# An attention kernel with a mixture of adapters behind it: one ring of four PSUM banks, casts tied to vector steps that read PSUM, and reordered first loads and mixture slots

## The chip, the cores and the metric

The kernel runs on one core of a Trainium2 chip. The metric is the device time of one execution in microseconds (us). Most executions of one kernel lie within 1 or 2% of each other. A run more than 1.5% above the fastest run of the same kernel is called slow and is left out of ratios. The profiled span is about 1.7 us shorter than the time of the same run, because the span runs from the first to the last instruction only.

Engines in the profile: PE is the matrix engine, PEld its weight load, DVE the vector engine, ACT the scalar engine, POOL the GpSimd engine and SP the engine that issues most transfers. A name with a q behind it (SPq, ACTq) is that engine's instruction stream issuing a transfer. The program keeps PE's results in tiles of PSUM, counted in banks, and its other tiles on the chip in SBUF. A transfer has landed when its semaphore tells that the data is there.

## The reference

The input is q, k and v of shape (8 batches, 8 heads, 576, 64), a table of biases, and the weights of a mixture of eight adapters.

```python
scores = q @ k.T / sqrt(64) + bias_table[bucket(|i - j|)]      # per batch and head
attn   = softmax(scores)
x      = (attn @ v), heads side by side                        # (4608, 512)
logits = x @ w_gate                                            # (4608, 8)
topk   = the two largest logits; w = softmax of these two
out    = x + sum over the two of  w_e * (x @ A[e]) @ B[e]      # rank 16
```

## The kernel before

The work is cut into 32 pairs (8 batches, four pairs of heads each) of five score groups. The bias is applied after the exponential, as a multiplication of a band of the probabilities ("band"). The 64 rows that 576 leaves over 512 are handled as "tails". Per pair: casts of k and q to bf16 on Pool, transposes on PE, scores on PE, exponentials on ACT, bands on DVE, values ("pv") on PE, and normalization into x on DVE. When the four pairs of a batch are done, the batch goes through the mixture while the next batch's attention runs: x is transposed by a DMA transfer (x to xT), then PE computes the logits (lp), the gate follows, and PE computes z and the output.

The parts that matter here, with cuts marked:

```python
scp = tile_pool("sc_ps",  bufs=2, space=PSUM)   # scores, two banks each
pvp = tile_pool("pv_ps",  bufs=1, space=PSUM)   # values: ONE buffer of two banks
acp = tile_pool("acc_ps", bufs=2, space=PSUM)   # transposes, mixture
...
def cast_kq(i, w, eng=None):                    # free-running on Pool
    ...
    nc.gpsimd.tensor_copy(o, s)
...
def norm(i, between):                           # frees the pv buffer at its end
    nc.vector.reciprocal(rc, at(acc, D, (SLOT, 5), (D1, 2)))
    between()                                   # a band
    nc.vector.tensor_tensor(rm, rc, mask, op=ALU.mult)
    nc.vector.tensor_tensor(xs[b][:, :, 2*hp:2*hp+2, :], <acc>, <rm>, op=ALU.mult)
...
def m_xdma(b):                                  # 512 KB, issued by SP in its order
    nc.sync.dma_start_transpose(out=xT, in_=xs[b][:, 0:4]...)
...
def mixture(b):
    i0 = HP * (b + 1) + 1                       # HP = 4 pairs per batch
    at_slot(0, 0, lambda: m_xdma(b))            # second pair of the next batch, group 0
    at_slot(1, 1, lambda: m_logits(...))        # six groups later
    ...
for i in range(NPAIR + 1):
    b, hp = divmod(i, HP)
    if hp == 0 and b + 1 < B:
        load_kq(b + 1, 0, H)                    # SP: k and q of the next batch, 1 MB each
        load_tails(b + 1)
    if b + 1 < B:
        load_v(b + 1, (hp,))                    # SP: four 64 KB transfers per pair
    ...
```

The softmax here doesn't subtract the row's maximum and nothing guards it: scores larger than these inputs give would overflow.

## Time and profile before

The median of the time before was 255.85 us over three runs. The page of the profile gives busy times per engine; the share is of the span. No engine is full, so the time is made of waits in turn.

The head of the page of the kernel before:

```profile
span 254.5 us, 6519 instructions
## 1 busy us (share of the span) xinstructions
PE 187.8 (74%) x2496; PEld 123.7 (49%) x2496; DVE 195.0 (77%) x483; ACT 162.7 (64%) x184; POOL 117.3 (46%) x229
```

What matters, read from the start of each pair's first exponential in the timeline:

| stretch | us |
|---|---|
| first exponential | 12.0 |
| start of pair 4 | 47.4 |
| pairs 4 to 30, each | 6.67 |
| from the start of pair 31 to the end | 26.9 |

The waits view lists who stood, for whom, in all, how often, and the longest. These are lines of the kernel before; PE waits for DVE to free the value buffer, for xT to land, and once for a long time for the first casts:

```profile
engine line waited for: us in total, times, longest us
...
PE pv L366 <- DVE x L392: 12.5, 13, 1.9
PE lp L438 <- DMA xT<-x: 11.9, 6, 3.1
...
PE kqps L287 <- POOL kqn L132: 10.0, 2, 7.3
```

The groups view by form gives busy time and mean of one instruction. On DVE, the three band sizes and the small multiplication rm:

```profile
L350 DVE TENSOR_TENSOR p<-p,M 128x768 bf16<-128x768 bf16 x64 | 38.4, 609 | 0.6 <-ACT p L335 0.5
L350 DVE TENSOR_TENSOR p<-p,M 128x512 bf16<-128x512 bf16 x64 | 29.3, 458 | 2.7 <-POOL M L223 2.7
...
L342 DVE TENSOR_TENSOR p<-p,M 128x256 bf16<-128x256 bf16 x32 | 18.5, 579 | 0.1
L391 DVE TENSOR_TENSOR rm<-rc,mask 128x10 f32<-128x10 f32 x32 | 10.2, 319 | 0.0
```

A band of 128x256 takes 579 ns on average, more than one of twice the size (458). The median of that form is 283 ns, so a few are very long. The timeline shows one; columns are start, duration, engine, line and operation. This is the one on DVE:

```profile
107.83 2.20 DVE L342 TENSOR_TENSOR p<-p,M 128x256 bf16<-128x256 bf16 x1
```
And this is the timeline of Pool over the same time, in the same columns:

```profile
107.58 0.64 POOL L132 CAST kqn<-kf 128x512 bf16<-128x512 f32 x1
108.14 0.63 POOL L132 CAST kqn<-qf 128x512 bf16<-128x512 f32 x1
108.69 0.63 POOL L137 CAST vn<-vf 128x512 bf16<-128x512 f32 x1
109.26 0.62 POOL L132 CAST kqn<-kf 128x512 bf16<-128x512 f32 x1
```

The band of 2.20 us lies over Pool's casts, which read SBUF. It ends at 110.03 us, while Pool's next cast (109.81 to 110.49 us) still runs. Take for each form of DVE instruction (with at least four of a form) the time above the form's 10th percentile: 27.4 us in all. The 62 instructions with two inputs in SBUF that overlap a Pool cast hold 23.7 us of it, the 45 with an input in PSUM that overlap one hold 0.05 us. This is what the change means to remove.

### The profile page before, as it was taken

How to read it: one execution, taken by the hardware profiler on the slowest of the kernel's cores; microseconds unless marked ns; L12 is line 12 of the kernel's file. 1: busy time of each engine (PE TensorE's matmuls, PEld its weight loads, DVE VectorE, ACT ScalarE, POOL GpSimd, SP SyncE). 2: the span in 40 equal slices, each digit the busy share in tenths (PEclk: the TensorE clock that was granted, in tenths of full speed). 3: DMA queues.
4: the chain of work that ended last, by engine and by line, in shares of the span. 5: the costliest groups of instructions: out<-in, count | busy, mean ns of one | idle time of the engine just before them, and what ended most of it. 6: DMA issues, size and time to landing. Idle time of an engine off the chain costs nothing.

```text
span 254.5 us, 6519 instructions
## 1 busy us (share of the span) xinstructions
PE 187.8 (74%) x2496; PEld 123.7 (49%) x2496; DVE 195.0 (77%) x483; ACT 162.7 (64%) x184; POOL 117.3 (46%) x229
## 2 busy tenths in 40 slices
PE   1324965888987596869879898879784997897650
PEld 1102543655754473546646574547353675556510
DVE  5215673899999579897997698988998599798771
ACT  3251874689987485777876586769676487895000
POOL 8599928671835254334743282714452282020100
PEclk9999998899999889899997797999889599999965
DMA  7999996997988697596987693886967301910616
GB/s 163 148 128 271 273 97 146 308 150 153 322 108 199 135 292 113 128 186 157 324 155 166 166 304 38 183 175 198 244 152 162 74 0 38 213 45 3 165 36 170
DMA packets 91830, 41.28 MB, mean 162 GB/s; under 512 B 69648, under 2 KB 87064, under 8 KB 91800
## 3 DMA queue, kind: packets, MB, share of 16 engines
q1 hardware_dynamic: 74392, 38.77, 61.5%
q0 software_dynamic: 17408, 2.10, 14.8%
q8 instruction: 19, 0.31, 0.5%
q14 instruction: 11, 0.09, 0.1%
HBM read 29.84 MB, written 9.45 MB: 154 GB/s over the span
## 4 chain that ended last, share of the span: by engine, by line
PE 43%; DVE 32%; DMA 13%; POOL 7%; issue 2%; ACT 1%; DVEq 0%; POOLq 0%; ACTq 0%
PE pv L366 17%; DMA xT<-x 11%; PE sc L323 9%; DVE p L350 6%; DVE x L392 6%; DVE o L517 5%; PE zp L487 3%; DVE p L342 3%; DMA tl<-in_q_dram 3%; DVE rm L391 3%; PE dl L513 3%; PE kqps L287 3%; DVE kqT L289 2%; POOL vn L152 2%; DVE tlT L298 2%
## 5 line engine op out<-in xcount | busy, mean ns | idle before, releaser
L335 ACT ACTIVATE p<-sc 128x1024 bf16<-128x1024 f32 x160 | 155.8, 1024 | 65.7 <-PE sc L323 36.1
L366 PE MATMUL pv<-vn,p 128*128 128x65 bf16 (+1 forms) x1152 | 68.2, 206 | 12.6 <-DVE x L392 12.5
L366 PEld LDWEIGHTS <-p 128*128 128x128 bf16 x1280 | 59.0, 104 | 37.4 <-issue 18.9
L350 DVE TENSOR_TENSOR p<-p,M 128x512 bf16<-128x512 bf16 (+1 forms) x128 | 66.2, 533 | 3.3 <-POOL M L223 2.7
L323 PE MATMUL sc<-kqT 64*128 64x512 bf16 x256 | 54.0, 419 | 2.8 <-ACT p L335 2.8
L287 PE MATMUL kqps<-ident,kqn 128*128 128x128 bf16 x256 | 21.6, 229 | 17.0 <-POOL kqn L132 10.0
L366 PE MATMUL pv<-vt,p 128*128 128x130 bf16 x128 | 29.8, 232 | 2.4 <-DVE p L342 2.4
L453 POOL TENSOR_TENSOR df<-lg,m 128x32 f32<-128x32 f32 (+1 forms) x12 | 3.5, 293 | 60.6 <-DVE lg L443 31.8
L287 PEld LDWEIGHTS <-kqn 128*128 128x128 bf16 x256 | 15.8, 101 | 24.6 <-POOL kqn L132 11.3
L392 DVE TENSOR_TENSOR x<-pv,rm 128x640 bf16<-128x640 f32 x32 | 26.4, 825 | 1.1
L289 DVE COPY kqT<-kqps 128x1024 bf16<-128x1024 bf16 x32 | 21.8, 682 | 7.0 <-PE kqps L287 7.0
L117 POOL DMA_DIRECT2D vt<-in_v_dram x16 | 9.8, 621 | 32.6 <-PE pv L366 32.6
L517 DVE TENSOR_TENSOR o<-dl,x 128x512 f32<-128x512 f32 x32 | 21.7, 687 | 3.7 <-PE dl L513 2.7
L323 PEld LDWEIGHTS <-kqT 64*128 64x128 bf16 x256 | 12.8, 94 | 18.5 <-issue 7.3
L132 POOL CAST kqn<-kf 128x512 bf16<-128x512 f32 x31 | 21.1, 680 | 0.1
L132 POOL CAST kqn<-qf 128x512 bf16<-128x512 f32 x31 | 20.5, 662 | 0.0
L137 POOL CAST vn<-vf 128x512 bf16<-128x512 f32 x28 | 20.5, 733 | 0.0
L342 DVE TENSOR_TENSOR p<-p,M 128x256 bf16<-128x256 bf16 x32 | 18.5, 579 | 0.1
L513 PE MATMUL dl<-Bb,zT 128*128 128x512 bf16 x32 | 14.2, 452 | 4.4 <-DVE kqT L289 2.5
L327 PE MATMUL sc<-kqT,tlT 128*128 128x512 bf16 x32 | 13.7, 427 | 0.0
L331 PE MATMUL sc<-tlT,kqT 128*128 128x128 bf16 x128 | 13.5, 233 | 0.0
L438 PE MATMUL lp<-Wb,xT 128*128 128x8 bf16 x128 | 4.5, 167 | 11.9 <-DMA xT<-x 11.9
(85 smaller groups left out, 209.3 us busy)
## 6 DMA issues: line engine op xcount, KB each, us to landing
out_dram<-o SPq DMA_DIRECT2D x64, 128.0 KB, 2.3
kf<-in_k_dram SPq DMA_DIRECT2D x7, 1024.0 KB, 5.9
qf<-in_q_dram SPq DMA_DIRECT2D x7, 1024.0 KB, 10.2
vf<-in_v_dram SPq DMA_DIRECT2D x112, 64.0 KB, 2.9
kf<-in_k_dram SPq DMA_DIRECT2D x4, 256.0 KB, 4.5
qf<-in_q_dram SPq DMA_DIRECT2D x4, 256.0 KB, 4.4
out_dram<-ot SPq DMA_DIRECT2D x8, 128.0 KB, 2.6
tl<-in_k_dram POOLq DMA_DIRECT2D x16, 32.0 KB, 6.8
```

The lines of the kernel that those rows point to most:

```text
L132: (eng or nc.gpsimd).tensor_copy(o, s)
L137: nc.gpsimd.tensor_copy(vns[b % 2][:, :, h, :D], vfs[b][:, :, h, :])
L287: nc.tensor.transpose(o[:, :, j, :], n[:, w, j], ident)
L289: nc.vector.tensor_copy(t, ps)
L323: nc.tensor.matmul(sc[:, h * 512:(h + 1) * 512], lhsT=t[s, 0, g * 128:(g + 1) * 128], rhs=t[s, 1, :], start=True, stop=True)
L335: nc.scalar.activation(p, sc, ACT.Exp, scale=scale)
L342: nc.vector.tensor_tensor(p[:, 384:640], p[:, 384:640], M4[:, hp, :], op=ALU.mult)
L350: nc.vector.tensor_tensor(o, o, Mh[:, :, x0 * 128:(x0 + b1 - b0) * 128], op=ALU.mult)
L366: nc.tensor.matmul(acc[:, sl * SLOT + o:sl * SLOT + o + n], lhsT=lhsT, rhs=rhs, start=start, stop=stop, skip_group_check=True)
L392: nc.vector.tensor_tensor(xs[b][:, :, 2 * hp:2 * hp + 2, :], at(acc, 0, (SLOT, 5), (D1, 2), (1, D)), rm.unsqueeze(3).to_broadcast((128, 5, ...
L513: nc.tensor.matmul(ps, lhsT=zT[:, t, :], rhs=Bb, start=True, stop=True)
L517: nc.vector.tensor_tensor(o[:, t], ps, xs[b][:, t].rearrange("p h d -> p (h d)"), op=ALU.add)
```

## The change: its intent and the diff

The intent has five parts.

1. Pool's casts of k, q and v are each made to wait for one DVE instruction whose successor reads PSUM, so that a cast does not meet a DVE step with two SBUF inputs.
2. The value buffer of two banks becomes two tiles of one bank each out of a ring of four, which transposes and mixture share. Each of the two is normalized and freed separately.
3. Scores are issued one group ahead of their exponential.
4. First loads: v of batch 0 is loaded by ACT and SP instead of Pool, casts of the first pairs go to DVE, and the exponential of the bias table and its transfer to memory (g_d, from which the bias matrix is read) come before the casts.
5. The mixture's slots move; all of one batch's tiles are handled together. xT is requested at group 4 of the first pair (before: group 0 of the second), the logits come at group 0 of the third pair (before: group 1). The distance stays six groups. The loads of a next batch are spread anew as well: eight of v's transfers instead of four in the first pair, and the tails of q one pair later than those of k (before: both in the first pair).

The core of the diff, with cuts:

```diff
-    pvp = tile_pool("pv_ps", bufs=1, space=PSUM)
-    acp = tile_pool("acc_ps", bufs=2, space=PSUM)
+    acp = tile_pool("acc_ps", bufs=4, space=PSUM)
...
+    def behind_dve(inst):
+        tc.add_manual_dep(inst.ins, dve.last.ins.name, ...,
+            reason="reads SBUF beside an instruction with an input in PSUM")
...
-    load_kq(0, 0, 2)
     nc.sync.dma_start(out=btT, in_=bias_table...)
+    load_kq(0, 0, 2)
+    load_v(0, (0, 1), nc.scalar)            # eight transfers issued by ACT
...
-    nc.sync.dma_start(out=g_d.ap(), in_=ge)
+    nc.scalar.dma_start(out=g_d.ap(), in_=ge)
+    cast_kq(0, 0, dve); cast_kq(0, 1, nc.scalar); cast_kq(1, 0, dve); cast_kq(1, 1, dve)
...
 def pv(i, sl):
-        if sl == 0:
-            pvs[i] = pvp.tile([128, 2 * S4], FP32, name="pv", tag="pv")
+        k = sl % 3
+        if k == 0:
+            pvs[(i, sl // 3)] = acp.tile([128, 3, 2 * D1], FP32, name="pv", tag="acc")
...
 def mixture(b):
-        i0 = HP * (b + 1) + 1
+        i0 = HP * (b + 1)
-            at_slot(0, 0, lambda: m_xdma(b))
-        at_slot(1, 1, lambda: m_logits(...))
+            at_slot(0, 4, m_xdma, b)
+        at_slot(2, 0, m_logits, b)
...
-            if b + 1 < B:
-                load_v(b + 1, (hp,))
+            for j in ((0, 1), (2,), (3,), ())[hp]:     # eight v transfers in the first pair
+                load_v(nb, (j,))
...
-                if g in (1, 2) and i + 2 < NPAIR:
-                    cast_kq(i + 2, g - 1)
+            if 3 <= i + 2 < NPAIR:
+                behind_dve(cast_kq(i + 2, 0))
+        if g == 2 and 3 <= i + 2 < NPAIR:
+            behind_dve(cast_kq(i + 2, 1))
+        if g == 4 and HP <= i + 1 < NPAIR:
+            behind_dve(cast_v(i + 1))
```

## The prediction

> **What bounds it now.** No single engine. The busy table gives DVE 195.0 us (77% of 254.5), PE 187.8, ACT 162.7. The ACT timeline: first exponential at 12.0 us, pair 4 of 32 only at 47.4; then 6.67 us a pair until pair 31 at 227.6; last pair and tail 26.9 us.
>
> Floors of one steady pair, summed from start-to-start times of uncontended instructions in the timeline: ACT five exponentials at about 0.92 = 4.8 us; PE 4.9 us at full clock (5.2 at the mean clock 0.92); DVE 4.9 us. So 6.67 holds about 1.5 us of stalls. From the waits and groups views:
> - PE stands behind the transposed x (about 12 us over 6 batches) and behind `x<-pv` freeing the single pv buffer (12.5 us).
> - DVE is held by Pool casts: the band 128x256 has median 283 ns but mean 579 and longest 2512 ns; 10-element rm has median 164, longest 1953. A 2.2 us band at 107.8 lies over four Pool casts. Summed excess over the 10th percentile of each form: about 26 us. This agrees with the Trainium skill, "SBUF — State Buffer", section "Who interferes with whom": a DVE instruction with two SBUF inputs contends with a GpSimd one that reads SBUF, and the loser blocks.
> - Start: PE waits 7.3 us for the kqn casts of pair 1, behind v loads on Pool.
>
> **What changes.**
> 1. Casts follow a DVE step whose successor reads PSUM (0.60 us kqT copy; 0.47 and 0.34 estimated for the two x halves). Casts of 0.61 fit under the first; the other two overrun by 0.15 and 0.3 us. I expect 26 us of excess to fall to 8 to 14.
> 2. The norm is split: one more reciprocal (0.12), two x instead of one (0.81 against 0.74): DVE +0.19 us per pair, +6 us in all.
> 3. PSUM ring of four: pv becomes two one-bank tiles, freed separately; the 12.5 us wait mostly goes, and DVE's wait for transposes falls.
> 4. Scores one group ahead of the exponential: ACT gaps shrink from 1.4 us a pair to about 0.8.
> 5. xT to logits remains about six groups; at 5.7 us a pair this just covers the 4.4 us transfer, so its wait falls from 2 to below 1 us per batch.
> 6. Start: casts of pairs 0 to 2 move from Pool to DVE (0.43 us each), v is loaded by hardware queues. ACT starts near 9 to 10 us and runs pairs 0 and 1 without stop; the bias matrix still lands near 16 to 17 us, behind 2.5 MB of loads. Pair 4 starts near 34 instead of 47.4: about 13 us.
>
> **Sum.** 34 + 27 x 5.75 = 189 for the start of pair 31, plus 25 for the end: 214 us. DVE sets the pair (5.05 floor, 0.4 contention, 0.3 waits), PE close behind. I estimate about 13 us from the start, 25 from the middle, 2 from the end.
>
> Predicted 214 us; 8 in 10: 204 to 227. Faster by over 2%: 0.96; within 2%: 0.03; slower: 0.01.
>
> **What would show it.** Band 256 mean near 300 ns and none over 1.2 us; DVE busy near 180; no `pv<-x` wait on PE; lp wait under 5 us; kqn releasers gone from the start, pair 4 at 32 to 37 us; ACT spacing median under 1.05 us. Wrong if casts still start late (Pool blocked by its own DMA descriptors), hitting bands; if a cast's late end delays the next transposes; if the granted clock drops as PE gets denser; if the bias matrix lands later than 18 us; or if the four-bank ring makes PE wait for DVE in strict order.

## The result, and the profile after

The changed kernel took 238.01 us (median of four runs, 237.07 to 238.95). The kernel before, on the same chip in the same rounds, took 257.74 us (254.53 to 285.35). The ratio of fast runs is 0.933, with a 95% interval of 0.924 to 0.942. A ratio is the mean time of one kernel's fast runs over that of the other's of the same rounds, so it is not quite the ratio of the medians quoted. The change makes the kernel faster by about 7%. The predicted 214 us was too low by 24 us, and the range (204 to 227) did not hold the result.

The head of the page after:

```profile
span 235.5 us, 6536 instructions
## 1 busy us (share of the span) xinstructions
PE 178.6 (76%) x2485; PEld 120.5 (51%) x2496; DVE 185.3 (79%) x540; ACT 160.7 (68%) x180; POOL 101.2 (43%) x195
```

The same stretches as before, beside the prediction, and beside a better version found later (e12, below). All are in us of the profiled span:

| stretch | before | predicted | after | e12 |
|---|---|---|---|---|
| start of pair 4 | 47.4 | 34 | 42.1 | 40.2 |
| 27 pairs | 180.2 (6.67 each) | 155.2 (5.75) | 166.0 (6.15) | 155.2 (5.75) |
| last pair and end | 26.9 | 25 | 27.3 | 27.7 |
| sum | 254.5 | 214 | 235.5 | 223.2 |

The miss in the span is 8 us at the start, 11 us in the middle and 2 us at the end. First, what went as planned. The groups view after (all DVE instructions carry the line of a helper, so the form tells them apart):

```profile
L82 DVE TENSOR_TENSOR p<-p,M 128x768 bf16<-128x768 bf16 x64 | 35.7, 559 | 0.0
...
L82 DVE TENSOR_TENSOR p<-p,M 128x256 bf16<-128x256 bf16 x32 | 12.4, 387 | 0.0
...
L82 DVE TENSOR_TENSOR rm<-rc,mask 128x4 f32<-128x4 f32 x32 | 5.3, 164 | 1.2
```

The band of 256 fell from 579 to 387 ns and its longest from 2512 to 573 ns; rm fell from 319 to 164 ns (it has 4 elements now instead of 10, but its median was 164 before too). Counted as above, the time over each form's 10th percentile fell from 27.4 to 8.4 us. What is left of it in the band of 256 are 12 of the 32, at about 570 ns: each met a cast of v that had begun 0.2 us before it.

The waits view after:

```profile
ACT p L350 <- PE sc L334: 30.7, 22, 6.3
...
PE lp L465 <- DMA xT<-x: 17.0, 6, 5.6
...
POOL M L238 <- DMA Mr<-g_d: 10.4, 1, 10.4
...
PE tps L306 <- DMA tl<-in_q_dram: 3.5, 1, 3.5
```

PE no longer waits for x to free the value buffer. But its wait for xT, which was to fall to a few microseconds, rose from 11.9 to 17.0 us. The longest is 5.6 us. ACT's 30.7 us behind scores are longest right there, since PE serves its steps in order and cannot start the scores behind the logits. The timeline of PE around that longest wait, which falls in batch 4's attention, with batch 3's logits:

```profile
124.37 0.39 PE L334 MATMUL sc<-kqT 64*128 64x512 bf16 x2
124.70 0.62 PE L297 MATMUL kqps<-ident,kqn 128*128 128x128 bf16 x8
130.89 0.69 PE L465 MATMUL lp<-Wb,xT 128*128 128x8 bf16 x20 [5.57 <-DMA xT<-x]
131.52 0.61 PE L334 MATMUL sc<-kqT 64*128 64x512 bf16 x2
```

PE ends the transposes at about 125.3 us and then stands until xT lands, 5.57 us. A pair of score matmuls took 0.39 us before it and takes 0.61 us after it. The table of stretches shows the granted clock (PEclk) for it; columns are busy times per engine, then the clock, the share of the DMA engines and GB/s:

```profile
124.00:126.00 2.00, 1.32 (x18) 0.81 (x15) 1.97 (x7) 1.87 (x3) 0.90 (x2) 1.00 0.75 150
...
128.00:130.00 2.00, 0.00 (x0) 0.00 (x0) 0.00 (x0) 0.00 (x0) 0.00 (x0) 0.50 1.14 208
...
134.00:136.00 2.00, 2.00 (x22) 1.72 (x21) 1.08 (x3) 0.94 (x1) 0.26 (x1) 0.50 0.86 152
...
138.00:140.00 2.00, 2.00 (x39) 1.67 (x37) 1.97 (x7) 1.96 (x3) 1.43 (x3) 1.00 1.11 341
```

The clock falls to 0.50 in the stand and is still 0.50 in the stretch to 136 us, five microseconds after PE has resumed. The Trainium skill, "TensorE: Matmul & The Clock Gate", section "Part 1: The HAM clock gate", says that the array falls to half its clock after an idle window of about 3.4 us and comes back after about as long busy, and that the window runs freely and isn't reset when a kernel starts. The clock record of the trace agrees with the window: all its changes lie on a grid of 3.41 us. Here the clock was at half from 127.06 to 137.30 us, three windows, the last 6.4 us of it with PE at work again. But PE need not stand for a whole window: the clock fell 1.7 us after PE had stopped, and the shorter stands of 2.23 and 2.88 us (batches 0 and 2 in the table below) were each followed by 3.41 us at half clock. So a stall of 5.6 us costs more than 5.6 us. The stalls of the kernel before cost clock too: its mean granted clock was 0.919, and 0.915 after the change.

The timeline of SP, which issues the transfers in program order, over the same stretch:

```profile
110.85 0.53 SPq L106 DMA_DIRECT2D kf<-in_k_dram  x1
111.48 1.56 SPq L106 DMA_DIRECT2D qf<-in_q_dram  x1
113.13 10.55 SPq L114 DMA_DIRECT2D vf<-in_v_dram  x8
123.78 2.21 SPq L542 DMA_DIRECT2D out_dram<-o  x4
126.10 2.58 SPq L432 DMA_TRANSPOSE xT<-x  x1
128.73 2.07 SPq L114 DMA_DIRECT2D vf<-in_v_dram  x4
```

x was done at 120.50 us. SP was then still issuing the next batch's v loads: eight of them took it 10.55 us, behind the 1 MB loads of k and q. Four such loads took 2.07 us after the transpose, so about 0.5 us each is what an issue costs when little is outstanding. The last of the eight was issued at 123.37 us, 0.02 us after q had landed; in the trace it uses the same semaphore as q's load, which is the eighth transfer before it. Then came four output transfers, and the transpose at 126.10 us. It landed at 130.84 us. The change had itself put eight v loads into the first pair of a batch, ahead of the transpose, where the kernel before had four per pair.

The same arithmetic for all batches. "Needed" is the time from x done to the first logits matmul; "covered" is that time less PE's idle time just before the logits, so it is the work that PE had to do meanwhile. All from the two traces, in us:

```
        before                        after
batch   needed  covered  PE waits     needed  covered  PE waits
0         5.97    5.26     0.71         6.98    4.75     2.23
1         7.75    4.69     3.06         5.78    4.83     0.95
2         7.56    5.57     1.99         7.43    4.55     2.88
3         7.56    6.26     1.30        10.39    4.82     5.57
4         7.31    5.57     1.74         5.17    4.55     0.62
5         8.46    5.37     3.09         9.52    4.83     4.69
mean      7.44    5.45     1.98         7.55    4.72     2.82
6         4.93    4.88     0.05         4.53    4.53     0.00
```

Batch 6 is a control that the program contains: there is no batch 8 to load behind it. There the transpose was issued 0.13 us after x was done and landed 4.36 us later, and PE did not wait. Wherever loads of a next batch are on their way, 5.2 to 10.4 us are needed. In batches 3 and 5 the time goes before the issue, 5.6 and 4.9 us after x was done (0.1 to 0.5 in the others); by then k and q had landed. In batches 0, 1, 2 and 4 the transfer is slow, 5.0 to 6.9 us. Beside it ran loads of v and 467 to 770 packets of tails, against at most 42 in batches 3, 5 and 6 (4.4 to 4.7 us) and at most 48 in the kernel before (4.4 to 4.7 us). Whether the tails are the reason is not shown: in e4, below, two transposes with no tails beside them took 5.4 and 5.8 us. The need stayed at 7.5 us, but the cover shrank by 0.7 us, because the pairs got faster.

The stall hides how fast the other pairs became. Six of the 27 pairs contain such a logits step (pairs 6, 10, 14, 18, 22 and 26). They took 56.7 us together, so 9.4 each; the other 21 took 5.21 us each, less than the predicted 5.75.

The start. The timeline of ACT in the first microseconds of the kernel before:

```profile
6.69 0.63 ACT L189 ACTIVATE ge<-g_sb 8x512 bf16<-8x512 f32 x1 [1.50 <-DVE g_sb L186]
12.02 1.02 ACT L335 ACTIVATE p<-sc 128x1024 bf16<-128x1024 f32 x1 [4.70 <-PE sc L323]
```
And of the kernel after (ACTq is ACT issuing a transfer):

```profile
0.74 7.87 ACTq L114 DMA_DIRECT2D vf<-in_v_dram  x8
8.65 1.28 ACT L200 ACT_TABLE_LOAD   x1 [8.65 <-DMA vf<-in_v_dram]
9.94 0.63 ACT L200 ACTIVATE ge<-g_sb 8x512 bf16<-8x512 f32 x1
...
14.49 2.96 ACT L350 ACTIVATE p<-sc 128x1024 bf16<-128x1024 f32 x3 [2.10 <-PE sc L334]
```

After the change, ACT spends 7.87 us on eight v loads. Issuing them takes 3.1 us of this. The rest is waiting: the program gives a new transfer the semaphore of an earlier one, of SP or of ACT, and the issue waits until that one has landed. ACT's fifth load was issued at 5.90 us, when SP's first load of q had landed (5.88), its sixth at 6.96 us, when SP's second load of k had (6.93). The activation table and the exponential that the bias matrix is made of (ge) come after them, so ge runs at 9.94 instead of 6.69 us. ACT's cast of q follows at 11.68 us, PE waits 4.9 us for it, and the first scores' exponential runs at 14.49 us instead of the predicted 9 to 10. The matrix landed at 18 us in its first part. Pool could copy its last part only at 24.81 us (the wait of 10.4 us above); behind that copy stood two casts and the last tails of q, for which PE waited 3.5 us. Pair 2 (counted from 0) took 11.1 us.

### The profile page after: what moved, and what is told of

Same layout as the page of the kernel before. It is cut to its first block, busy times and chain, and to the rows that moved or that the text cites. A ratio compares the mean times of both kernels' runs of the same rounds, so it can differ in the third digit from the quotient of the medians.

```text
span 235.5 us, 6536 instructions
## 1 busy us (share of the span) xinstructions
PE 178.6 (76%) x2485; PEld 120.5 (51%) x2496; DVE 185.3 (79%) x540; ACT 160.7 (68%) x180; POOL 101.2 (43%) x195
## 4 chain that ended last, share of the span: by engine, by line
DVE 37%; PE 28%; DMA 20%; issue 4%; ACT 4%; SPq 2%; POOL 2%; POOLq 0%; DVEq 0%
DVE p L82 12%; DMA xT<-x 12%; PE pv L380 10%; DVE x L82 7%; PE sc L334 7%; DVE o L82 4%; ACT p L350 4%; DMA tl<-in_q_dram 2%; DVE rc L82 2%; DMA vf<-in_v_dram 2%; PE tps L306 2%; PE kqps L297 2%; DMA qf<-in_q_dram 2%; DVE kqT L82 2%; PE zp L511 2%
## 5 line engine op out<-in xcount | busy, mean ns | idle before, releaser
L350 ACT ACTIVATE p<-sc 128x1024 bf16<-128x1024 f32 x160 | 153.3, 1034 | 39.8 <-PE sc L334 30.7
L82 DVE TENSOR_TENSOR p<-p,M 128x512 bf16<-128x512 bf16 (+2 forms) x160 | 73.6, 475 | 0.0
L380 PE MATMUL pv<-vn,p 128*128 128x65 bf16 (+1 forms) x1152 | 62.7, 203 | 1.7 <-DVE p L82 1.7
L380 PEld LDWEIGHTS <-p 128*128 128x128 bf16 x1280 | 53.9, 102 | 12.1 <-issue 11.2
L297 PE MATMUL kqps<-ident,kqn 128*128 128x128 bf16 x256 | 21.6, 230 | 14.2 <-DVE kqn L82 7.9
L152 POOL CAST vn<-vf 128x512 bf16<-128x512 f32 x28 | 17.3, 620 | 30.8 <-DVE p L82 15.7
L82 DVE TENSOR_TENSOR x<-pv,rc 128x384 bf16<-128x384 f32 x32 | 17.8, 557 | 1.1
L82 DVE RECIPROCAL rc<-pv 128x6 f32<-128x6 f32 x64 | 11.7, 182 | 4.3 <-PE pv L380 4.0
L465 PEld LDWEIGHTS <-xT 128*128 128x128 bf16 x144 | 4.4, 99 | 19.6 <-DMA xT<-x 18.1
L343 PEld LDWEIGHTS <-kqT 128*128 128x128 bf16 x128 | 10.2, 101 | 7.4 <-issue 3.0
L82 DVE COPY tlT<-tps 128x1024 bf16<-128x1024 bf16 x8 | 5.5, 690 | 10.3 <-PE tps L306 10.2
L82 DVE TENSOR_TENSOR x<-pv,rm 128x256 bf16<-128x256 f32 x32 | 13.3, 417 | 0.0
## 6 DMA issues: line engine op xcount, KB each, us to landing
qf<-in_q_dram SPq DMA_DIRECT2D x7, 1024.0 KB, 10.5
```

What stands on the lines that cost most here:

```text
L82: self.last = f(*a, **kw)
L152: return (eng or nc.gpsimd).tensor_copy(vns[b % 2][:, :, h, :D], vfs[b][:, :, h, :])
L297: nc.tensor.transpose(o[:, :, j, :], n[:, w, j], ident)
L343: nc.tensor.matmul(sc[:, o:o + 128], lhsT=t[:, 0, j * 128:(j + 1) * 128], rhs=tt[:, 1, hp, :], start=True, stop=True, skip_group_check=True)
L350: nc.scalar.activation(p, scs.pop(n), ACT.Exp, scale=scale)
L380: nc.tensor.matmul(acc[:, k, o:o + n], lhsT=lhsT, rhs=rhs, start=start, stop=stop, skip_group_check=True)
```

## The experiments

Eighteen versions ran, all as edits of the changed kernel, each in three rounds or more beside the kernel before, whose median lay between 254.8 and 257.0 us in these rounds. The texts name theories by letters in some places: the main theory is that the distance from x to the logits is too short for what stands between them; theory B is that the DMA engines are full with v's small packets; S2 is that the landing of the bias matrix sets the start; Q and L are that SP's order and its reused semaphores hold the transpose. Two cautions hold for all of them. Groups of runs were made on different chips, so ratios are the safer comparison. And the start varies from profile to profile: in seven runs that don't edit it (e1, e2, e4, e6, e7, e13, e17) pair 4 began at 42.7 to 45.7 us, so the change's 42.1 is at the low edge, and 3 us there show nothing.

### The stall: more distance, and the transfers

**e1: logits and everything behind them one pair later**, for batches 0 to 5.

```diff
+            late = 5 if b < B - 2 and di >= 2 else 0
-            events.setdefault(5 * (i0 + di) + g, []).append((f, a))
+            events.setdefault(5 * (i0 + di) + g + late, []).append((f, a))
```

> Edit: in batches 0 to 5 the gate scores of the mixture (logits) and everything of the mixture behind them come one pair (five groups) later; nothing else moves. Theory (the missing 25 us of the middle are PE standing in program order before the logits for the transposed x): PE's idle time before lp falls from 17 us to under 2, the pairs of the third place in a batch fall from 5.9 to 13.8 us to about 5 to 6, the granted clock in them stays near 1, and the time falls from 238 to 212 to 220. Rival A (the DMA queues or the DVE are full, so the wait only moves): the lp wait goes, but waits for kf, qf, tl or a DVE stall take its place and the time stays above 230. Rival B (the low granted clock in these pairs is a cause of its own): the third pairs stay above 7 us with a clock of 0.6 to 0.8.

Measured: 229.74 us (228.60 to 230.66), ratio 0.899 [0.889, 0.908], against 0.933 for the change. PE's wait for xT fell from 17.0 us in six to 1.3 us in one, although the transpose was still issued up to 6.95 us after x was done. So the distance is what PE's wait depends on. The gain is 8 us, not the 20 that the excess of the six pairs suggested, and the forecast of 212 to 220 us was missed. The pairs that had stood took 5.4 to 6.9 us (pair 18: 9.0), together 18 us less than in the change. The other 21, which now hold the mixture's work that had followed the stall, took 7 us more (5.54 instead of 5.21 each). So the 27 pairs average 5.74 us instead of 6.15. PE also waits 8.4 us for q's tails in the transposes of the tails (3.5 in the change). Pair 4 starts 2.8 us later, which is within the spread named above.

**e2: the next batch's loads one pair earlier**, so that they have landed when x is done.

```diff
-            if hp == 0: alloc_loads(nb); load_kq(nb, 0, H)
-            for j in ((0, 1), (2,), (3,), ())[hp]: load_v(nb, (j,))
+        lb, lp = divmod(i + 1, HP); lb += 1
+            if lp == 0: alloc_loads(lb); load_kq(lb, 0, H)
+            load_v(lb, (lp,))
```

> Edit: from batch 2 on, the loads of a batch's k, q and v are issued one pair earlier (before the last pair of the batch before the previous one ends), so that the big k and q loads are ten groups, not four, ahead of the x transpose on the SP queue; the logits stay six groups behind the transpose. Theory Q (the transpose is late because it stands on SP behind the issue of loads, and slow because it shares the DMA engines with them): issue after x falls from 5.6 and 4.9 us in batches 3 and 5 to under 1, issue-to-logits from up to 6.9 to under 5 us, PE idle before lp from 17 to under 4 us in all, time 216 to 225. Theory D (the distance of six groups is too short anyway at this pace): the issue is prompt, but PE still idles 0.5 to 1 us before every lp; time about 222 to 228. If neither queue nor load matters, nothing changes: 236 to 240.

Measured: 238.09 us (235.20 to 240.70), ratio 0.924 [0.910, 0.937]; the profiled run was a slow one. PE's wait for xT was 14.2 us, with issue delays of 3.99 and 4.06 us in batches 3 and 5. The loads stood earlier in the program but not in time: on SP an output transfer stood ahead of them and waited for its data. This run does not tell the theories apart.

**e6: k and q two pairs earlier, v one pair earlier.**

```diff
+        if g == 0 and hp == 2 and b + 2 < B:
+            alloc_loads(b + 2); load_kq(b + 2, 0, H)
```

> Edit: from batch 2 on the k and q loads are issued two pairs earlier (in the third pair of the batch before the last), ahead of the output DMA that held SP in the run with loads one pair early, and the v loads one pair earlier, four per pair. The logits stay six groups behind the x transpose. Theory L (SP issues in order, and each load through a hardware queue reuses the semaphore of the one eight before it, so the eighth DMA after a 1 MB q load waits for that load, and the transpose waits behind it): in batches 3 and 5 the issue of the transpose after x falls from 5.6 and 4.9 us to under 1; PE idle before lp falls from 17 us to under 6 in all; time 225 to 232. Rival (the transpose is held by something else on SP, the output DMA's wait for DVE for example): the delays of 4 to 5 us stay.

Measured: 242.53 us (236.20 to 245.25); three of its four runs were slow, the profiled one too, so there is no ratio. Now the transpose was issued 0.1 to 0.7 us after x was done, except in batch 5 (3.56). But its time from issue to logits was 5.4 to 8.8 us, PE's wait was still 10.6 us, and PE waited 7.7 us for Pool's casts of k and q. A wait at the issue had become a longer transfer.

**e17: k and q of batches 2 to 7 issued by Pool** instead of SP. This takes them out of SP's order without moving them in the program. In time it moves them: Pool issued them 5.3 to 5.8 us before x was done, where SP in the change had issued them 9.3 to 16.4 us before.

```diff
-            nc.sync.dma_start(
+            (nc.sync if b < 2 else nc.gpsimd).dma_start(
```

> Edit, from the changed kernel: the k and q loads of batches 2 to 7 are issued by Pool, at the same place in the program, so that SP's loads no longer use again a semaphore of a 1 MB load and the transpose does not stand behind them on its queue. Theory L (that semaphore holds SP 4 to 6 us in batches 3 and 5): issue after x under 1 us in batches 2 to 5, PE idle before lp from 17 us to under 7 us, no wait for kqn, time 222 to 231. Rival (the queue does not matter, the transfers share the DMA engines anyway): lp waits fall by less than 4 us, time within 3 us of 238. Third: Pool, issuing 1 MB descriptors, delays its casts; then POOL is late for kqn and the time is 235 or above though the lp wait is gone.

Measured: 264.22 us (261.72 to 265.73), ratio 1.044 [1.029, 1.059], slower than the kernel before. From x done to the issue it was now 0.46 us at most, as intended. The transfers view of e17 (the transfer, its issuer, count, median us from issue to landing):

```profile
xT<-x SPq DMA_TRANSPOSE x7, 10.5
```
The waits view of e17:

```profile
PE lp L465 <- DMA xT<-x: 36.2, 6, 7.0
```

The transpose now took 10.5 us instead of 5.0, and PE waited 36.2 us. So the 2 MB of k and q delay the transpose on either path: ahead of it in SP's order, or beside it on the DMA engines. How much of the 10.5 us comes from the issuer and how much from the later issue, this run does not tell apart. The Trainium skill, "DMA: Bandwidth & Descriptors", section "Issuing engines are not separate DMA queues", says that transfers of all issuers run on the same 16 engines and interleave. This run agrees, with 10.5 against 4.36 us for batch 6, which has no loads beside it.

**e9: v in runs of 1 KB** instead of 256 bytes, a wrong result (relative error 0.10), to test whether the DMA engines are full with small packets. **e10: the same and the logits later.** Their outputs are wrong, which doesn't matter for the times.

```diff
-        vr = v[b, :, :S4, :].rearrange("h (t p j) d -> j t p h d", t=4, j=4)
+        vr = v[b, :, :S4, :].rearrange("h (p j) d -> p h (j d)", j=4)
```

> Wrong result on purpose: the v loads read whole runs of 1 KB instead of 256 B, so the rows of v are in a wrong order; bytes, number of DMAs and their places on the queues, casts and all computing stay. Of the DMA packets' summed time (206 us over 16 engines in a span of 235) the 256 B packets of v take 72 us. Theory B (the DMA engines themselves are full, so every saving elsewhere is given back to the loads, as the runs with an earlier start showed: pair 7 started at 59 to 62 us in nearly all of them): v's packet time falls to 30 to 40 us, the x transposes land in 4.4 to 5 us, issue delays of 4 to 5 us in batches 3 and 5 shrink, PE idle before lp falls below 6 us in all, pair 7 starts before 56 us, and the time falls to 208 to 224. Rival Q (SP's order and the semaphores used again every eight loads hold the transposes, not the bytes): delays and lp waits stay within 20% and the time is above 232.

> Wrong result on purpose as in the run with 1 KB v loads, and the logits one pair later too. Theory: what is left after both waits are taken away is the engines' own pace: no pair after the fifth above 6.5 us, lp wait zero, pairs at 5.2 to 5.5 us, time 203 to 214. If it is not faster than 1 KB v loads alone, the slots no longer matter once the DMA engines have room. If it is near 229, the later logits and not the DMA engines bound the earlier run.

Measured: e9 took 239.63 us (236.85 to 244.34), ratio 0.949 [0.929, 0.969]. The packets' time per DMA engine fell from 206 to 183.5 us, yet PE waited 16.3 us for xT, as in the change (17.0). (The text's 72 us are all packets of 256 B. In e9, 14,336 of the 47,104 are left, as many as seven transposes of 512 KB make, so v's own took about 50 us, and about 29 as runs of 1 KB.) So theory B falls as it was put. e10 took 227.77 us (225.01 to 228.54), ratio 0.900 [0.867, 0.934], like e1: the logits' distance again did the work, with no wait for xT although the transpose was issued up to 10.8 us after x was done.

### The stall: loads behind the transpose

**e13: k and q of the next batch but one issued right behind the transpose**, v one pair later. **e14** adds earlier tails, **e15** the start of e8 as well, and **e16** is e14 with the logits two groups later.

```diff
-            if hp == 0:
+            if i == 0:
                 alloc_loads(nb); load_kq(nb, 0, H)
-            for j in ((0, 1), (2,), (3,), ())[hp]:
+            for j in ((), (0, 1), (2, 3), ())[hp]:
+        if g == 4 and hp == 0 and 0 < b < B - 1:      # after the mixture's slot
+            alloc_loads(nb); load_kq(nb, 0, 2); load_kq(nb, 2, H)
# e14, e15, e16 also:
-        if g in (1, 3) and hp < 3 and nb < B:
+        if g in (1, 3) and hp in (0, 2) and nb < B:
             load_tail(nb, hp, g // 2)
+            if hp == 0: load_tail(nb, 1, g // 2)
# e16 also: late = 2 groups in the mixture
```

> Edit, from the changed kernel: from batch 2 on the k and q loads stand on SP behind the x transpose, not before it (heads 0 and 1 first, then 2 to 7), and the v loads one pair later. Slots, casts and all computing stay. Theory L (the transpose is late because it stands on SP behind eight v loads, of which the last reuses the semaphore of the 1 MB q load and waits for its landing): issue after x below 1.2 us in every batch from 1 on, landing 4.4 to 4.7 us after issue, PE idle before lp from 17 us to under 5 us in all, no third pair above 7 us apart from batch 0's, time 216 to 226. Rival (six groups are too short at this pace whatever the queue): lp waits of 1 us or more per batch stay though the issue is prompt. Third possibility: k and q now land too late for the casts and PE waits for kqn instead; then the lp wait goes but the time stays above 230.

> As the run with loads behind the transpose, and the k and q tails of a batch all in its predecessor's first pair. With the transpose no longer waiting, the 3 us that the early tails save in the start should now be kept, not given back at the first logits as they were in the run with tails first alone: 212 to 222, 3 us or more below the run with loads behind alone. If it equals that run, the start's gain is again given back.

> As the run before, and the sixteen v loads of batch 0 spread over three issuing engines with the bias matrix ahead of the later k and q loads. First exponential at 10 us, pair 4 at 34 to 38; 210 to 221. If the start is still given back at pair 7, equal to the run before.

> As the run with loads behind and tails, and the logits with all behind them two groups later in batches 0 to 5. If six groups are too short at a pace of 5.2 us a pair even with a prompt transpose (Theory D), this gains 2 to 6 us over it; if the queue was all (Theory L), it is within 1.5 us of it.

Measured: e13 248.35 us (246.69 to 249.46), ratio 0.969 [0.959, 0.979]; e14 239.67 us, 0.934 [0.926, 0.943]; e15 239.51 us, 0.934 [0.925, 0.942] (its profiled run a slow one); e16 248.67 us, 0.971 [0.962, 0.980]. In e13 the transpose was issued within 0.14 us of x in batches 0 to 5 but one (2.47), and PE's wait for xT fell to 4.6 us. The wait moved: PE waited 13.6 us for Pool's casts of k and q, and Pool's casts of v waited 23.4 us for transfers. In e14 PE's wait for xT is 3.1 us and that for the casts 14.4 us; in e16 the first is gone and the second is 29.9 us. Loads that come after the transpose come too late for the casts. The 2 MB have to land in one batch's time in any order; only the consumer that waits changes.

### The start

**e3: all of v's first loads on SP**, so that ACT is free.

```diff
-    load_v(0, (0, 1), nc.scalar)
+    load_v(0, (0, 1))
```

> Edit: the first eight v loads of batch 0 are issued by SP, not by ACT. ACT spent 7.9 us issuing them, so its exponential of the bias table ended at 10.6 us and its cast of q at 12.4. Theory S1 (the start is set by the first exponential): the first exponential moves from 14.4 to about 10 us, pair 4 starts about 4 us earlier (38), and the time falls by 3 to 5 us. Theory S2 (the start is set by the landing of the bias matrix and by Pool behind it; the DMA engines are full until then): the first exponential moves to about 10 us but the bias matrix still lands at 17 to 19 us, pair 4 starts at 41 to 43 us as before, and the time stays within 1.5 us.

Measured: 240.22 us (237.41 to 243.23), ratio 0.932 [0.919, 0.945]. The first exponential came at 12.5 us instead of 14.5, but pair 4 at 44.0 instead of 42.1, within the spread. The chain of the start in e3 shows why; these are pieces of the chain of what ended last, with start and duration:

```profile
6.37 3.00 DMA g_d<-ge
9.39 0.33 SPq L114
...
21.57 0.43 SPq L213
22.05 4.16 DMA Mr<-g_d
```

The transfer of the small table (g_d) that the bias matrix is read from ended at 9.37 us. From there SP issued 26 transfers one after another, up to 0.7 us each; the bias matrix's last part was issued at 22.05 us and landed at 26.2 us. The landing of that matrix, with the time of issuing, sets this start; ACT's own issuing alone does not. (In the change the last link is what Pool issues behind the matrix, the tails of q: see e5.)

**e5: the q tails of batch 1 earlier.** **e8: these, and only four of v's loads on ACT, eight on Pool, four on SP; k and q of heads 4 and 5 behind part of the bias matrix, those of heads 6 and 7 behind all of it.**

```diff
# e5
+            if (nb, hp) == (1, 0): load_tail(1, 1, g // 2)
# e8 also
-    load_v(0, (0, 1), nc.scalar)
+    load_v(0, (0,), nc.scalar)
+    load_v(0, (1, 2), nc.gpsimd)
-    load_v(0, (2, 3))
-    load_kq(0, 4, 6)
+    load_v(0, (3,))
...                                            # in and behind the bias matrix's loop
-            load_kq(0, 6, H)
+            load_kq(0, 4, 6)
+    load_kq(0, 6, H)
```

> Edit: Pool issues batch 1's q tail loads in pair 0, before it waits for the bias matrix, not in pair 1 behind that wait. Nothing else. In the changed kernel PE stood 3.5 us (3.7 and 3.6 in other runs) in pair 2 for these loads, because Pool issued them only at 27.5 to 29.3 us, behind the bias copies that waited for the matrix until 24.8. Theory (this wait is on the path of the start): PE's wait for the q tail in the first 45 us goes to 0, pair 4 starts at 37 to 40 us instead of 42 to 44.8, time 233 to 236. Rival (the start is DMA-bound, so another load takes its place): pair 4 at 41 us or later, time 237 to 240.

> Edit: only the loads before pair 2. The sixteen v loads of batch 0 are spread over three issuing engines (four on ACT, eight on Pool, four on SP), the bias matrix is issued on SP before the k and q loads of heads 4 to 7, and batch 1's q tails go first as in the run with tails first. Theory (in the start SP's own issue time, 0.45 us for each of some 40 DMAs, stands before the bias matrix, as the chain of the run with v on SP shows: SP from 9.4 to 22.1 us): the first part of the bias matrix lands at 13 to 15.5 us instead of 18, the last at 19 to 22 instead of 24.8, pair 4 starts at 34 to 38 us instead of 42 to 44.8, and the time falls to 229 to 234. Rival (the start is bound by the DMA engines' bytes): the matrix lands at 17 us or later whatever the order, and the time stays above 235.

Measured: e5 241.13 us (235.33 to 241.34; three of four runs slow, so no ratio), e8 236.13 us (233.92 to 237.76), ratio 0.924 [0.909, 0.939], against 0.933 [0.924, 0.942] for the change, so no gain is shown. In e8 the first exponential came at 10.1 us and pair 4 at 37.2 us, five microseconds earlier than in the change. Yet pair 7 started at 61.2 us, as in the change (60.6). Pair 5 took 8.6 us instead of 4.5, with PE 2.5 us behind Pool's casts. In batch 0 x was done early, at 43.2 us, and the transpose issued 6.93 us later, in the middle of the loads; PE's wait for it grew from 2.23 to 3.20 us, and pair 6, with the first logits, took 10.4 us instead of 8.9. In e5 it is the logits alone: pair 4 at 38.8, pair 7 at 61.5 us, with PE's wait at 5.02 us. An earlier start was given back by the end of the pair with the first logits.

### Tie and ring

**e4: the casts without the tie.** **e7: two banks for values and two for all else**, instead of one ring of four.

```diff
# e4
     def behind_dve(inst):
-        tc.add_manual_dep(inst.ins, dve.last.ins.name, ...)
+        pass
# e7
-    acp = tile_pool("acc_ps", bufs=4, space=PSUM)
+    pvp = tile_pool("pv_ps", bufs=2, space=PSUM)
+    acp = tile_pool("acc_ps", bufs=2, space=PSUM)
```

> Edit: the semaphore that ties the Pool casts to a DVE step is taken out; order and everything else stay. The data dependencies stay, so it is free of races. Theory (the tie is what took the summed DVE excess from about 27 us to 8): the excess of the DVE bands rises to 15 to 25 us, single bands of over 1.2 us come back, and the time rises by 2 to 8 us. Rival (the order in the program alone keeps casts apart; the tie does nothing, or costs by delaying transposes): the excess stays under 11 us and the time is within 1.5 us or lower.

> Edit: the four PSUM banks are no longer one ring: two banks for the two pv tiles, two for everything else; the same number of banks and the split norm stay. Theory (splitting the values into two one-bank tiles freed PE; which pool they come from matters little): PE's wait for x stays under 2 us and the time is within 2 us of 238. Rival (the ring of four is what keeps PE running, because two banks for transposes and mixture are what it had before): PE waits again for kqT, o, zT or for x, 5 us or more in all, and the time rises by 3 to 10 us.

Measured: e4 243.41 us (243.08 to 244.10), ratio 0.953 [0.945, 0.960], 5.4 us above the change's median. The groups view of e4:

```profile
L82 DVE TENSOR_TENSOR p<-p,M 128x768 bf16<-128x768 bf16 x64 | 42.2, 661 | 0.0
...
L82 DVE TENSOR_TENSOR rm<-rc,mask 128x4 f32<-128x4 f32 x32 | 7.4, 232 | 1.2
```

The large band rose from 559 to 661 ns and rm from 164 to 232 ns; the summed excess was 21.0 us against 8.4, 17.0 us of it in instructions with two SBUF inputs that overlap a cast. Four of the 32 bands of 256 took over 1.2 us, the longest 1.66 us. So the tie does what it was meant to do. The excess of 12.6 us costs 5 us of time, since part of it lies where DVE would have waited anyway (this last is an inference). e7 took 239.81 us (236.05 to 241.80), ratio 0.945 [0.931, 0.960]; by its interval it overlaps the change's 0.924 to 0.942. Which pool the banks come from does not show. That values take two separately freed tiles of one bank is common to both, and PE's wait of 12.5 us for x is gone with it.

### Combinations

**e12: logits one pair later (e1) and the k and q tails all requested in the first pair of a batch**, in time for their transposes. **e11** is e1 with the start of e8, these tails and later mixture weights. **e18** is e12 with k and q on Pool (as e17).

```diff
# e12, beyond e1
-        if g in (1, 3) and hp < 3 and nb < B:
+        if g in (1, 3) and hp in (0, 2) and nb < B:
             load_tail(nb, hp, g // 2)
+            if hp == 0:
+                load_tail(nb, 1, g // 2)
```

> Right result; a candidate to beat both: logits one pair later, the loads of the start spread as in the start run, all k and q tails of a batch in its predecessor's first pair, and the mixture's weights two pairs later (their A matrix is 4096 packets of 32 B, 8 us of DMA time in the crowded start). Theory B: the start gains little by itself because the DMA engines are full, but with the logits later nothing stands for the x transpose any more, so the start's gain is kept: 220 to 227. Rival: as with the early start alone, the gain is given back: 228 to 231.

> Right result: logits one pair later and all k and q tails of a batch in the first pair, without the other changes of the start. The wait for q tails (8.4 us in the run with later logits alone, 3.6 in the start and up to 3.6 in batch 3) goes: 222 to 228. If the time is no better than 229.7, the tails were not on the path.

> Right result; as the best so far (logits one pair later, early tails: 225.7 us), and k and q loads by Pool. If the loads on SP still cost there (the waits for lp of 2.8, 0.4 and 1.3 us in batches 3 to 5 and the slow third pairs): 217 to 224. If nothing waits for the transpose any more: 224 to 227. If Pool's issue delays casts: above 228.

Measured: e12 225.68 us (224.41 to 227.02), ratio 0.897 [0.884, 0.911], correct. This is the lowest median, 12 us under the change, but it comes from a chip on which the kernel before took 254.8 us, not 257.7; by the ratios the gain over the change is about 9 us. Against e1 (0.899 [0.889, 0.908]) the ratio shows no difference. The traces agree as to the middle, 155.2 us against 155.0 in e1; what the tails bring is at most an earlier pair 4 (40.2 against 44.9 us). e11 took 226.34 us (224.85 to 228.87; profiled slow), ratio 0.898 [0.879, 0.917], the same within the intervals: with the logits later, the start of e8 still brings nothing that can be measured. e18 took 230.62 us (228.13 to 233.91; no ratio). In e18 10.5 to 13.8 us went by between the issue of the transpose and the logits without a wait of PE for it, but PE waited 7 us for tails and 6 us for Pool's casts. The head of the page of e12:

```profile
span 223.2 us, 6539 instructions
## 1 busy us (share of the span) xinstructions
PE 177.1 (79%) x2496; PEld 118.3 (53%) x2496; DVE 188.4 (84%) x540; ACT 161.4 (72%) x180; POOL 103.9 (47%) x195
```
And two lines of its waits view:

```profile
ACT p L350 <- PE sc L334: 14.9, 17, 3.0
...
PE lp L465 <- DMA xT<-x: 4.5, 3, 2.8
```

ACT's wait for scores is half of the change's 30.7 us. The cover is now 10.3 to 10.9 us per batch, and only batch 3, which needs 13.5, still stands for more than 2 us. The mean granted clock is 0.955 instead of 0.915. The pair is 5.75 us.

## Why the prediction was right or wrong

**Right in direction and in these mechanisms.** The kernel became faster, though by 7% rather than the 16% that 214 us would have been. The excess of DVE fell from 27.4 to 8.4 us (predicted 8 to 14), and e4 shows that the tie does it. It is the conflict that the Trainium skill names in "SBUF — State Buffer", section "Who interferes with whom". The trace agrees: the band of 2.20 us over four casts before, none above 0.6 us of its form after, and nearly all of the excess in instructions with two SBUF inputs beside a cast. No wait of PE for x to free the value buffer is left. DVE's busy time is 185.3 us (predicted near 180). The pairs without a logits step take 5.21 us, faster than the 5.75 of the prediction. The band of 256 at 387 ns missed "near 300", since 12 of 32 met a cast of v; its median is 283 in both kernels. DVE's wait for the transposes of k and q, which was to fall, did not (7.0 us before, 8.6 after). The median spacing of exponentials told nothing, since it was below 1.05 us in the kernel before too (1.02; 0.92 after).

**Wrong in step 5**: "xT to logits remains about six groups; at 5.7 us a pair this just covers the 4.4 us transfer, so its wait falls from 2 to below 1 us per batch". The cover measured 4.5 to 4.8 us, and it does just cover 4.4 us, in batch 6. (Six groups at 5.7 us a pair would be 6.8 us; PE has part of them behind it when x is done.) What was mis-sized is the term that it was compared with. The 4.4 us are the transfer alone, read from a kernel whose pairs were slow enough for the loads to be nearly over. From x done to the logits the kernel before needed 7.4 us on average, and this could be read from its trace: x done, then 2.9 to 4.0 us to the issue in most batches, then 4.4 to 4.7. After the change the need was 7.5 us, and the wait was 2.8 us per batch instead of below 1. The wait rose because the kernel became faster. The longest stall put PE's clock to half for 10.2 us, 6.4 of them at work; the prediction named the clock only as falling when PE gets denser, but it fell because PE stood.

By numbers: had the pairs taken 5.21 us throughout, 27 of them would have taken 141 us; they took 166. The 25 us of the six pairs are not all loss: in e1, without the stall, 18 us of them went, and 7 us came back in the other pairs. Taking the stall away brought 8 us (e1) by the medians and about 9 by the ratios (e1 and e12 alike). The 5.74 and 5.75 us a pair of e1 and e12 are the predicted figure.

**Wrong in step 6**: "ACT starts near 9 to 10 us and runs pairs 0 and 1 without stop; the bias matrix still lands near 16 to 17 us". ACT started at 14.5 us; the term left out is its own v loads, 7.87 us, of which 4.8 us are waits for earlier transfers. The matrix landed at 18 us in its first part, and Pool had the last part at 24.8 us. Pair 4 started at 42.1 instead of 34 us. PE's waits for Pool's casts went as predicted (10.0 to 1.4 us), but it then waited 12.8 us for the first casts of DVE and ACT (4.6 before). Removing ACT's issuing alone (e3) brought nothing by pair 4; e8 brought 5 us there, and lost it again by the first logits, probably because a start that comes early meets the same loads. So even a right step 6 would not have given its 13 us without a right step 5.

**The end** was 27.3 instead of 25 us; no run looked into it.

**Settled and open.** Settled: the stall comes from the distance between x and its logits, against a need of 5 to 10 us that exists only when the next batch's loads are around (e1, e10, e12, e17, batch 6). Settled too: other orders of the loads turn it into another wait (e6, e13 to e16), and v's packets are not the cause (e9). Open: why the transfer takes 5.0 to 6.9 us where it was issued at once in the change, whether tails, v's loads or something else; why 7 of the 18 us that e1 takes out of the six pairs come back in the others, for which work put off by a stall is an argument and not a measurement; and whether the earlier tails of e12 are worth anything.

## What to carry to other kernels

When a consumer sits a fixed number of steps behind an asynchronous transfer, compare its distance not with the transfer's duration but with the whole time from data ready to data landed, under the load that is there, and do this again with the step times after the change: a speedup elsewhere shortens the cover and can make a small wait grow. If the data is not urgent, give the consumer more steps before touching the order of the loads; here one pair more brought 8 to 9 us, while every other order only moved the wait. A gain at the start counts only after the first place where all streams meet.

## What the Trainium skill lacked or had wrong

- "DMA: Bandwidth & Descriptors" gives a bandwidth for the DMA transpose (261 GB/s in one case) and says that one next to ordinary transfers needs nothing. That holds for correctness here. It lacks the latency under load: 512 KB took 4.36 us from issue to landing with no loads beside it (about 120 GB/s, worked out from both), up to 6.9 us beside loads of v and tails, and 10.5 us (median) when k and q, issued by another engine and later, were still landing.
- The same page, section "Issuing engines are not separate DMA queues", calls the issuing engine's time usually small beside the transfer. It lacks that an issue takes longer when large loads are outstanding: the first seven of SP's issues behind a 1 MB load took 0.6 to 2.2 us each, later ones 0.45 us. And it lacks the waits between issues where transfers take turns with few semaphores: eight issues held ACT for 7.87 us, of which 3.1 us were issuing.
- "TensorE: Matmul & The Clock Gate", section "Part 1: The HAM clock gate", puts the fall to half clock after at least one idle window of about 3.4 us. The grid of 3.41 us is in the trace, but less than an idle window was enough: a stand of 2.23 us, in a window of which PE was busy for 1.18 us, was followed by 3.41 us at half clock. The return took 6.4 us of work, which the free-running window of the page allows.
- "SBUF — State Buffer", section "Who interferes with whom", was right about who blocks. It gives the factor of one measurement (DVE 6.8 times slower), but not what this sums to in a kernel: one band of 0.28 us took 2.20 us over a row of casts, and tying the casts to steps with a PSUM input took the summed excess from 21.0 to 8.4 us (e4 against the change).
